# Four edits to a planned one-core kernel: an eviction's engine, three ring buffers, the split of the warming matmuls, and a new order of the work

## The chip, the core and the metric

The kernel runs on one core of one Trainium2 chip. A core has five engines, each with a queue of its own that it works through in order: TensorE (PE: matrix multiplications, with its weight loads, PEld), VectorE (DVE), ScalarE (ACT), GpSimdE (POOL) and SyncE (SP, which here only issues transfers). [...] A matrix multiplication writes to one of eight accumulator banks (PSUM); ACT or DVE then copies the bank to on-chip memory, which is called an eviction here.

The metric is the time of one execution on the device in microseconds. Of the kernel before, three runs gave 339.36, 339.56 and 339.56 us: median 339.56.

## The reference

Two layers, each a long convolution and a gated feed-forward block, on one sequence of 2048 rows with 512 columns. What is computed:

```python
def A(q, k, v, shift_k, ssm_k, ssm_D):        # convolution
    k_shift = sum(k shifted down by j rows * shift_k[:, j] for j in 0..3)
    kv = k_shift * v
    y  = causal convolution over all 2048 rows of kv with ssm_k   # by FFT
    return q * (y + kv * ssm_D)

def B(x, w_gate, w_up, w_down):               # feed-forward, F = 1792
    return (silu(x @ w_gate) * (x @ w_up)) @ w_down

x = A_q
x = x + A(layernorm(x), ...);  x = x + B(layernorm(x), ...)
x = x + A(layernorm(x), ...);  x = x + B(layernorm(x), ...)
```

All inputs are bfloat16. The convolution's `y` does not depend on `x`, so it is computed once and used in both layers.

## The kernel before

**Tiles and stages.** The sequence is cut into four blocks `c` of 512 rows, a block into two halves `h` of 256 rows. A unit is `(layer, c, h)`: one half of one block in one layer, sixteen in all. For each unit a prologue normalises, multiplies with `y`, adds to `x`, normalises again and transposes the result to `zT`; `ffn` then multiplies `zT` with `wg_sb` and `wu_sb` (line 400 of the profile, written by `mm`), evicts on ACT (`sg`, `hr`, `ht`), multiplies on DVE, and multiplies with `wd_sb` (line 1200).

**The convolution** is done with matrix products in place of an FFT. For block 0, `transpose_h` turns the filter `hn` (line 567), `transpose_k` turns `kn` to `kTb` (line 456), `half` takes the filter's spectrum `ev` in eight matrix products of two terms each (slots a, b, c, d, two parts each), whose banks are evicted at line 509 (ACT) or 512 (DVE); `shift_mul` multiplies `kTb` by the diagonal matrices `dg` (the four taps, made at lines 1362 and 1366) and DVE multiplies the result by `v` (line 614); `direct` takes the spectrum `X0` of that (line 548). DVE forms `G0` from `ev` (lines 535, 537), then the products `t`, `Z` and sums `m` (lines 732, 736, 873), TensorE turns them back (line 879), and the first prologue follows (lines 990 to 1013), at whose end the first feed-forward product can start. `EVE` is the string that names the engine of each eviction of `half(hs, ev, ...)`: its first four letters belong to slots a and c, part 0 and 1 each.

**Strassen units.** In the five units named in `STRASSEN` some groups of the down product are done with seven products in place of eight (`seven`, line 1075). It needs sums of quarters of `wd_sb`, made once by `weight_sums` (lines 1035 and 1039): `wsa`, `wsb`, `wsc`, three of the eleven slots of the ring `s8` from then on.

**What sets the order.** Nothing is issued in the order in which the code is written. Each operation is put on a list with its engine, a cost and its readers and writers (`Plan.add`). `ORDER` is a table with one rank for each of the 1721 operations, written out by hand or by a search that is not in the kernel; `Plan.order` sorts by it, and each engine gets its operations in that order. `Plan.walk` then steps through the sorted list with the costs and gives every operation a planned start. The planned starts decide two things only: which slot of a ring a buffer gets, and where the warming matmuls go. No operation waits for its planned time on the chip; it waits for its operands and its slot.

**Warming matmuls** (`wm`, line 1485) multiply ones, so that TensorE is busy before its first data land. `Plan.issue` puts a run of them ahead of an operation of TensorE whose planned start is before 6.0 and over 0.5 after the planned end of the one before, as many as fit at 0.106 each, and then corrects the first run so that there are `WARM`, 33, in all:

```python
n = int((start - max(t, 0.3)) / 0.106)
...
fill[0][3] += WARM - sum(f[3] for f in fill)
```

In the code, the taps' transposes (line 1348) follow at 3.02 after the start (0.42 for the issue, 2.6 for landing) with a cost of 0.25, and the filter's (line 567) at 0.62 + `LH0`.

**Transfers** are issued by SP in the order of the table too: the filter, `k`, `v`, `x`, the weights, the inverse table `inv` by a transposing transfer, and later the transposes of `z` and of `hr`.

Of the kernel before, what the change touches and what calls it, by code (L numbers as in the profile page):

```python
# [33 lines left out]
LH0 = 4.0  # L34
# [7 lines left out]
EVE = "ADADAAAA"  # L42
# [80 lines left out]

PASSES, WARM, FETCH, PHASE, TOOK = 4, 33, 256, 173, 1.1

NS = 8
BLOCKS = [("C", 0, 1), ("C", 1, 1), ("C", 2, 1), ("C", 3, 1),
# [1389 lines left out]
```

## Time and profile before

| | us |
|---|---|
| median of three runs | 339.56 |
| the profiled execution's own time | 340.1 |
| its span, first to last instruction | 338.3 |
| TensorE busy | 333.9 |
| VectorE busy | 299.8 |
| ScalarE busy | 265.0 |
| GpSimdE busy | 34.5 |

The profiled execution took 340.1 us, of which 1.8 us lie around its span, and it is 0.54 us above the median. A busy time is the time in which at least one instruction of that engine was under way. Consecutive matrix products overlap: one of 512 columns is shown with 0.38 us, but the next can start 0.216 us later. So a busy TensorE is not one that issues without a gap; gaps are read from the starts of consecutive rows. In rows of the timeline stand start, length, engine, line, operation, tiles, and how many instructions of that kind are merged; in square brackets the idle time of the engine before it, and what ended it. `PEld` rows are weight loads, rows with a `q` are issues of transfers.

### The profile page before, as it was taken

The numbers are of one execution on the slowest core, as the hardware profiler recorded it, in microseconds if no ns is written. First come the engines' busy times: TensorE is split into PE (matmuls) and PEld (weight loads), VectorE is DVE, ScalarE is ACT, GpSimd is POOL, SyncE is SP. The second block draws the span as 40 slices with busy tenths as digits, with TensorE's granted clock in tenths as the row PEclk, the third lists the DMA queues.
The fourth block names the chain that finished last, engine by engine and source line by source line (L and its number), as shares of the span: only waits on it lengthen the run. The fifth ranks groups of instructions, "written<-read, shape, count | busy, mean of one in ns | idle before, by whom it ended". The sixth has DMA issues, their size and how long they took to land.

```text
span 338.3 us, 5940 instructions
## 1 busy us (share of the span) xinstructions
PE 333.9 (99%) x2172; PEld 205.7 (61%) x2172; DVE 299.8 (89%) x508; ACT 265.0 (78%) x543; POOL 34.5 (10%) x48
## 2 busy tenths in 40 slices
PE   9999999999999999999999999999999999999996
PEld 8665865645454564745444564644546587867884
DVE  7899999999779997999999999989997967977465
ACT  6989999999987477989999886989765555566473
POOL 4010011003100000132030000101200010100000
PEclk9999999999999999999999999999999999999999
DMA  7999501443355336381333263510504230203201
GB/s 266 341 290 365 75 0 33 84 107 90 64 125 93 81 79 155 62 159 32 62 48 67 57 107 116 105 34 16 96 16 96 56 85 2 48 17 78 64 3 62
DMA packets 77992, 31.59 MB, mean 93 GB/s; under 512 B 69765, under 2 KB 75786, under 8 KB 77962
## 3 DMA queue, kind: packets, MB, share of 16 engines
q1 hardware_dynamic: 77808, 31.13, 39.8%
q8 instruction: 17, 0.28, 0.3%
q14 instruction: 13, 0.11, 0.1%
q10 hardware_dynamic: 154, 0.07, 0.1%
HBM read 12.33 MB, written 2.10 MB: 43 GB/s over the span
## 4 chain that ended last, share of the span: by engine, by line
PE 87%; ACT 7%; DVE 5%; issue 1%; POOL 0%; DVEq 0%; POOLq 0%
PE pf L400 50%; PE pd L1200 17%; PE ps L1075 7%; PE ps L400 7%; PE ps L548 2%; ACT jk L922 2%; PE wm L1485 1%; PE ps L879 1%; ACT sg L1113 1%; ACT hr L1114 1%; ACT X L509 1%; PE pt L567 1%; DVE t L746 1%; DVE m L630 1%; DVE Z L750 1%; DVE t L742 1%
## 5 line engine op out<-in xcount | busy, mean ns | idle before, releaser
L400 PEld LDWEIGHTS <-zT 128*128 128x128 bf16 x528 | 51.5, 98 | 59.4 <-DMA zT<-z 0.9
L400 PE MATMUL pf<-wu_sb,zT 128*128 128x512 bf16 x264 | 65.0, 379 | 0.0
L400 PE MATMUL pf<-wg_sb,zT 128*128 128x512 bf16 x264 | 64.9, 379 | 0.0
L1200 PE MATMUL pd<-wd_sb,sg 128*128 128x512 bf16 x200 | 49.4, 379 | 0.0
L1113 ACT ACTIVATE sg<-pf 128x512 bf16<-128x512 f32 x66 | 38.7, 604 | 11.4 <-PE pf L400 10.3
L400 PE MATMUL pf<-zT,wg_sb 128*128 128x256 bf16 x368 | 46.7, 273 | 0.0
L1114 ACT CAST hr<-pf 128x512 bf16<-128x512 f32 x66 | 38.2, 591 | 9.6 <-PE pf L400 9.0
L400 PE MATMUL pf<-zT,wu_sb 128*128 128x256 bf16 x368 | 45.4, 273 | 0.2 <-ACT zT L1013 0.2
L742 DVE TENSOR_TENSOR t<-X,G 128x4096 bf16<-128x4096 bf16 x18 | 41.0, 2280 | 0.1
L400 PEld LDWEIGHTS <-wg_sb 128*128 128x128 bf16 x368 | 36.0, 98 | 8.0
L400 PEld LDWEIGHTS <-wu_sb 128*128 128x128 bf16 x368 | 36.0, 98 | 7.1 <-issue 0.5
L1173 ACT ACTIVATE sg<-pf 128x512 bf16<-128x512 f32 x46 | 27.5, 606 | 10.9 <-PE pf L400 9.7
L1177 ACT CAST ht<-pf 128x512 bf16<-128x512 f32 x46 | 27.3, 599 | 10.8 <-PE pf L400 10.4
L889 POOL TENSOR_TENSOR rstd<-mv,nhalf 128x2 f32<-128x2 f32 x20 | 18.5, 928 | 160.3 <-DVE mv L899 160.3
L1200 PEld LDWEIGHTS <-sg 128*128 128x128 bf16 x200 | 19.6, 98 | 21.5
L1200 PE MATMUL pd<-wd_sb,ht 128*128 128x512 bf16 (+1 forms) x126 | 29.1, 369 | 0.0
L898 DVE BATCH_NORM_STATS2 bst<-xc 128x6 f32<-128x512 bf16 x40 | 26.4, 682 | 0.5
L1180 DVE TENSOR_TENSOR ht<-ht,sg 128x512 bf16<-128x512 bf16 (+1 forms) x31 | 16.7, 546 | 9.5 <-ACT sg L1173 6.2
L889 POOL TENSOR_TENSOR rstd<-ve,nhalf 128x2 f32<-128x2 f32 x12 | 12.4, 1032 | 112.3 <-ACT ve L926 112.3
L1120 DVE TENSOR_TENSOR hr<-hr,sg 128x1024 bf16<-128x1024 bf16 x27 | 18.4, 681 | 4.3 <-ACT hr L1114 2.3
L509 ACT ACTIVATE X<-ps 128x512 bf16<-128x512 f32 x32 | 18.8, 611 | 2.2 <-DVE Z L746 1.1
L1200 PEld LDWEIGHTS <-ht 128*128 128x128 bf16 x126 | 12.3, 98 | 12.8 <-ACT z L945 0.3
(143 smaller groups left out, 525.7 us busy)
## 6 DMA issues: line engine op xcount, KB each, us to landing
hn<-in_A_ssm_k_dram SPq DMA_DIRECT2D x4, 512.0 KB, 4.0
vt<-in_A_v_dram SPq DMA_DIRECT2D x4, 512.0 KB, 6.0
xc<-in_A_q_dram SPq DMA_DIRECT2D x4, 512.0 KB, 5.3
out_dram<-xc SPq DMA_DIRECT2D x15, 128.0 KB, 1.8
wg_sb<-in_B_w_gate_dram SPq DMA_DIRECT2D x1, 1792.0 KB
wu_sb<-in_B_w_up_dram SPq DMA_DIRECT2D x1, 1792.0 KB, 7.9
wd_sb<-in_B_w_down_dram SPq DMA_DIRECT2D x1, 1280.0 KB, 13.2
sg<-hr SPq DMA_TRANSPOSE x66, 2.4
```

What stands on the lines that cost most here:

```text
L400: nc.tensor.matmul(o, lhsT=lhsT, rhs=rhs, start=(n == 0), stop=(n == len(terms) - 1))
L509: add("ACT", act(D), lambda: nc.scalar.activation(out=view(), in_=ps.t[:], func=ACT.Copy, scale=scale), r=[ps], w=[(buf, keys)], conv=conv)
L742: dve(8 * D, lambda t=t, part=part: nc.vector.tensor_mul(out=t.t[:], in0=x.t[:, :, part:part + 1, :].to_broadcast((P, R, 2, D)), in1=g.t[: ...
L889: add("POOL", cost, lambda: nc.gpsimd.tensor_tensor(out=rstd.t[:], in0=var(), in1=nhalf.t[:].to_broadcast((P, n)), op=ALU.pow), r=reads + ...
L898: add("DVE", 0.6, lambda st=st, i=i: nc.vector.bn_stats(out=st.t[:, 0:6], in_=xs[c].t[:, i, :]), r=[(xs[c], (i,))], w=[st])
L1075: nc.tensor.matmul(bank.t[:, half_ * C:(half_ + 1) * C], lhsT=lhsT(i), rhs=rhs(i), start=(first and i == 0 and half_ == 0), stop=(last and ...
L1113: add("ACT", act(D), lambda ps=ps, dst=dst, o=o, which=which: nc.scalar.activation(out=rows(dst, o), in_=ps.t[:], func=ACT.Silu) if which ...
L1114: out=rows(dst, o), in_=ps.t[:], func=ACT.Silu) if which == "g" else nc.scalar.copy(out=rows(dst, o), in_=ps.t[:]),
L1120: dve(n * W, lambda: nc.vector.tensor_mul(out=hr.t[:], in0=hr.t[:], in1=sg.t[:]), [sg], [hr], due=(unit, k / pairs, 0.0, "h"))
L1173: add("ACT", act(D), lambda ps=ps, o=o, sg=sg: nc.scalar.activation(out=sg.t[:, o:o + 2, :], in_=ps.t[:], func=ACT.Silu), r=[ps], w=[(sg, ...
L1177: add("ACT", act(D), lambda ps=ps, o=o, ht=ht: nc.scalar.copy(out=ht.t[:, o:o + 2, :], in_=ps.t[:]), r=[ps], w=[(ht, (o // 2,))], due=(uni ...
L1200: nc.tensor.matmul((pds[o] if not cs.start else pds[HP]).t[:, cs], lhsT=ht.tiles(q, o), rhs=wt["d"].t[:, ft, cs], start=(ft == std0 and no ...
```

## The change

1. `LH0` goes from 4.0 to 3.85, and `Plan.walk` counts an operation of TensorE that starts before `RAMP`, 5.4, at up to 1.92 times its cost. Both are numbers of the plan; through it they set where the warming matmuls go (33 in all, as before) and which slots buffers get.
2. `EVE` goes from `ADADAAAA` to `AAADAAAA`: the eviction of slot a, part 1 of the filter's spectrum goes from DVE (line 512) to ACT (line 509).
3. `weight_sums` writes its five results to five buffers: two in the rings `h` and `k` (one slot each, earlier used for the filter and for `kTb`), one in `hs`, one in `dg` (a ring of one slot now, for the diagonals), and one in `s8`. The last two take sums of even and of odd tiles in place of first and second halves. `seven` reads them under new names.
4. `ORDER` is replaced. Of 523 operations of TensorE 437 stand at another position in its queue, of 508 of DVE 399, of 497 of ACT 433, of 43 of POOL 18 and of 150 of SP 91. The sets of operations are the same, but for the eviction of item 2.

```diff
-LH0 = 4.0
+LH0 = 3.85
...
-EVE = "ADADAAAA"
+EVE = "AAADAAAA"
...
 ORDER = [
-    1, 64, 179, 187, 2, 5, 0, 11, 15, 3, 4, 8, 14, 34, 36, 9, 7, 10, 6, 13, 19, 18, 17, 16, 20, 25, 27, 45, 51, 41, 47, 48, 31, 55, 33, 42, 32, 39,
...
+    6, 53, 44, 124, 2, 7, 4, 12, 24, 1, 3, 0, 17, 18, 30, 10, 8, 11, 9, 15, 27, 21, 19, 16, 20, 29, 32, 34, 40, 31, 56, 78, 22, 46, 14, 36, 23, 49,
...
 ]
...
-PASSES, WARM, FETCH, PHASE, TOOK = 4, 33, 256, 173, 1.1
+PASSES, WARM, FETCH, PHASE, TOOK, RAMP = 4, 33, 256, 173, 1.1, 5.4
...
             o.end = o.start + o.cost
+            if o.eng == "PE" and o.start < RAMP:
+                o.end += 0.48 * min(1.92 * o.cost, RAMP - o.start)
...
-    plan = Plan({"h": 1, "k": 1, "v": 1, "hs": 1, "x": 2, "y": 2, "s8":11, "n": 2, "jk": 1, "dn": 1, "ks": 2, "z": 3, "zT":3,
+    plan = Plan({"h": 1, "k": 1, "v": 1, "hs": 1, "dg": 1, "x": 2, "y": 2, "s8":11, "n": 2, "jk": 1, "dn": 1, "ks": 2, "z": 3, "zT":3,
...
-    dg = whole("dg", [P, KD, KS, P], parts=KD * KS)
+    dg = new("dg", "dg", [P, KD, KS, P], parts=KD * KS)
...
-        a = ws["14"] = new("s8", "wsa", [P, 2, NF // 2, C], parts=2)
-        b = ws["3"] = new("s8", "wsb", [P, NF // 2, C])
-        c = ws["67"] = new("s8", "wsc", [P, NF, C])
...
+        a0, a1 = (new(ring, "wsa", [P, NF // 2, C]) for ring in ("h", "k"))
+        b = new("hs", "wsb", [P, NF // 2, C])
+        c0, c1 = (new(ring, "wsc", [P, NF // 2, C]) for ring in ("dg", "s8"))
+        ws.update({"1": a0, "4": a1, "3": b, "6": c0, "7": c1})
...
```

The heads of the queues, as they follow from the two tables:

| queue | before | after |
|---|---|---|
| TensorE | taps; filter rows 3, 0, 1, 2; `kn` parts 3, 1, 2, 0; spectrum c, c, a, a; `dg` products and spectrum b, d | taps; filter rows 2, 0, 1, 3; `kn` 0, 1, 2; spectrum b, a, c, d; `kn` 3; `dg` products and the other four of the spectrum |
| DVE, from the taps' copies on | tapT, tapF, phases, three `dg`, a row of `hs`, both negated tables, a row of `hs`, five `dg`, `kTb`, ev, `kTb`, ev, G, four `vt` | tapF, phases, negated table, `dg`, negated table, tapT, two rows of `hs`, six `dg`, `kTb`, `dg`, `kTb`, ev, G, four `vt` |
| ACT, around the spectrum | two `kTb`, ev, `dg`, ev, `dg`, two ev, sums of `x` | `kTb`, ev, `kTb`, ev, `dg`, three ev, sums of `x` |
| POOL | iota, iota, `ident`, zeros of `kTb`, ... | iota, zeros of `kTb`, iota, `ident`, ... |
| SP, after `wd_sb` part 1 of 2 | `wd_sb` part 2, `xc` of block 1, `hn` of block 2, `kTb` of block 2, ...; `vt` of block 2 much later | `hn` and `vt` of block 2, `wd_sb` part 2, `xc` of block 1, `kTb` of block 2, ... |

Up to the first feed-forward product TensorE has the same operations to do in both tables, in another order. In both, the last ten operations of TensorE, the last seven of DVE and the last three of ACT are the same.

More of the change, by code (lines that the diff above doesn't have):

```diff
@@ L1027, in weight_sums @@
         lo, hi = slice(0, C), slice(C, D)
-        a = ws["14"] = new("s8", "wsa", [P, 2, NF // 2, C], parts=2)
-        b = ws["3"] = new("s8", "wsb", [P, NF // 2, C])
-        c = ws["67"] = new("s8", "wsc", [P, NF, C])
-        for out, keys, x0, x1, op in (
-                (lambda: a.t[:, 0], [(a, (0,))], lambda: ev(lo), lambda: od(hi), ALU.add),
-                (lambda: b.t[:], [b], lambda: ev(hi), lambda: od(hi), ALU.subtract),
-                (lambda: a.t[:, 1], [(a, (1,))], lambda: od(lo), lambda: ev(lo), ALU.subtract)):
-            dve(NF // 2 * C, lambda out=out, x0=x0, x1=x1, op=op: nc.vector.tensor_tensor(out=out(), in0=x0(), in1=x1(), op=op),
-                [wd], keys)
-        for n in range(2):
-            sl = slice(n * NF // 2, (n + 1) * NF // 2)
-            dve(NF // 2 * C, lambda sl=sl: nc.vector.tensor_tensor(out=c.t[:, sl], in0=wd.t[:, sl, lo], in1=wd.t[:, sl, hi], op=ALU.add),
-                [wd], [c])
+        a0, a1 = (new(ring, "wsa", [P, NF // 2, C]) for ring in ("h", "k"))
+        b = new("hs", "wsb", [P, NF // 2, C])
+        c0, c1 = (new(ring, "wsc", [P, NF // 2, C]) for ring in ("dg", "s8"))
+        ws.update({"1": a0, "4": a1, "3": b, "6": c0, "7": c1})
+        for out, x0, x1, op in ((a0, lambda: ev(lo), lambda: od(hi), ALU.add), (b, lambda: ev(hi), lambda: od(hi), ALU.subtract),
+                                (a1, lambda: od(lo), lambda: ev(lo), ALU.subtract), (c0, lambda: ev(lo), lambda: ev(hi), ALU.add),
+                                (c1, lambda: od(lo), lambda: od(hi), ALU.add)):
+            dve(NF // 2 * C, lambda out=out, x0=x0, x1=x1, op=op: nc.vector.tensor_tensor(out=out.t[:], in0=x0(), in1=x1(), op=op),
+                [wd], [out])
     def strided(src, off, dims):
@@ L1060, in seven @@
         for bank, rd, terms in (
-                (e, [ht, ws["14"], ws["3"]], (
-                    (0, lambda i: ht.tiles(2 * i + 1, 1), lambda i: ws["14"].t[:, 1, f0 + i]),
+                (e, [ht, ws["4"], ws["3"]], (
+                    (0, lambda i: ht.tiles(2 * i + 1, 1), lambda i: ws["4"].t[:, f0 + i]),
                     (1, lambda i: ht.tiles(2 * i, 0), lambda i: ws["3"].t[:, f0 + i]))),
@@ L1066, in seven @@
                     (1, lambda i: cb.t[:, 1, i], lambda i: wd.t[:, 2 * (f0 + i), 0:C]))),
-                (r, [(cb, (1,)), ws["67"]], (
-                    (0, lambda i: cb.t[:, 3, i], lambda i: ws["67"].t[:, 2 * (f0 + i) + 1]),
-                    (1, lambda i: cb.t[:, 2, i], lambda i: ws["67"].t[:, 2 * (f0 + i)]))),
-                (o, [(cb, (2,)), ws["14"]], (
-                    (0, lambda i: cb.t[:, 4, i], lambda i: ws["14"].t[:, 0, f0 + i]),))):
+                (r, [(cb, (1,)), ws["6"], ws["7"]], (
+                    (0, lambda i: cb.t[:, 3, i], lambda i: ws["7"].t[:, f0 + i]),
+                    (1, lambda i: cb.t[:, 2, i], lambda i: ws["6"].t[:, f0 + i]))),
+                (o, [(cb, (2,)), ws["1"]], (
+                    (0, lambda i: cb.t[:, 4, i], lambda i: ws["1"].t[:, f0 + i]),))):
             def go(bank=bank, terms=terms):
```

126 rows, old and new, of the table ORDER are left out of this document.

## The prediction

> **What bounds the kernel now.** I read the page's sums and chain first, then busy time by stage, then the timeline wherever TensorE is not issuing.
>
> ```profile
> span 338.3 us, 5940 instructions
> ...
> PE 333.9 (99%) x2172; PEld 205.7 (61%) x2172; DVE 299.8 (89%) x508; ACT 265.0 (78%) x543; POOL 34.5 (10%) x48
> ...
> PE 87%; ACT 7%; DVE 5%; issue 1%; POOL 0%; DVEq 0%; POOLq 0%
> ```
>
> The last of these rows is the chain that ended last: TensorE holds 87% of it. The change removes no matmul, so all it can win is time in which TensorE does not issue, or issues slowly. By stage (stretch, its length, then busy time and count of PE, PEld, DVE, ACT, POOL, granted clock, DMA):
>
> ```profile
> 8.00:12.00 4.00, 4.00 (x45) 2.87 (x44) 3.30 (x7) 3.94 (x9) 0.00 (x0) 1.00 1.04 398
> 26.40:33.20 6.80, 6.33 (x57) 3.72 (x56) 6.25 (x16) 6.80 (x15) 0.78 (x1) 1.00 1.08 364
> 255.00:338.30 83.30, 80.27 (x640) 62.35 (x637) 58.61 (x147) 46.84 (x88) 4.66 (x6) 1.00 0.22 50
> ```
>
> From 8 to 12 ScalarE is the fullest engine beside TensorE; from 26.4 to 33.2 TensorE loses 0.47 even by busy time; in the last 83 us it lacks only what lies at the very end. Now the start, from the timeline and two answers on single tiles (shortest, median and longest matmul in ns; issue to landing of the filter's loads):
>
> ```profile
> 0.77 2.40 PE L1485 MATMUL wm<-const-bfloat16-1.0 128*128 128x128 bf16 x21 [0.77 <-PEq L1503]
> 3.10 0.29 PE L1348 MATMUL pt<-ident,tapR 4*128 4x4 bf16 x4
> 3.32 1.46 PE L1485 MATMUL wm<-const-bfloat16-1.0 128*128 128x128 bf16 x12
> 4.58 1.91 PE L567 MATMUL pt<-ident,hn 128*128 128x128 bf16 x16
> 6.29 1.40 PE L456 MATMUL pt<-ident,kn 128*128 128x128 bf16 x16
> 10.79 3.07 PE L400 MATMUL ps<-dg,kTb 128*128 128x128 bf16 x52
> ...
> L456 PE MATMUL pt<-ident,kn x16: 219/219/311, 6.3 to 7.5; 128*128 128x128 bf16 x16
> ...
> DMA to landing us min/median/max: 3.6/5.7/7.8
> ```
>
> The granted clock is 1.00 in every stretch, yet the pitch is not: sixteen filter transposes take 1.91, less the last one's 0.31 is 1.60 for 15 steps, 0.107 each; 52 later ones take 3.07, less 0.22 is 2.85 for 51 steps, 0.056. TensorE runs at half rate early. The `kn` row holds the change: 1.40 less 0.22 is 1.18 for 15 steps, some seven slow and eight fast, so it comes near 7.0. Sixteen plus seven useful matmuls are slow by 0.051 each: 1.2 us lost. The filter landed at 0.74 + 3.6 = 4.34; TensorE took it up at 4.58.
>
> The end of the head, where the first feed-forward product waits, and the unit of pitch (the last row, from the chain: 20 matmuls of 512 columns in 4.32, 0.216 each):
>
> ```profile
> 25.43 2.31 PE L879 MATMUL ps<-m,inv 128*128 128x512 bf16 x9
> 31.10 0.38 PE L879 MATMUL ps<-m,inv 128*128 128x512 bf16 x1
> 31.78 0.72 PE L1008 MATMUL ptz<-ident,z 128*128 128x128 bf16 x8 [0.31 <-DVE z L950]
> 32.44 0.60 PE L400 MATMUL ps<-vt,fwd 128*128 128x512 bf16 x2
> 33.22 1.91 PE L400 MATMUL pf<-zT,wu_sb 128*128 128x256 bf16 x16 [0.17 <-ACT zT L1013]
> ...
> 65.11 4.32 PE pd L1200 x20
> ```
>
> Nine in 2.31 need 8 x 0.216 + 0.38 = 2.11: 0.20 idle. From 31.10 + 0.216 to 31.78 are 0.46, after eight transposes (0.45) 0.21, after two matmuls (0.43) 0.35. The head loses 1.2 us of issue, and ends when `zT` is there: a chain over VectorE from `ev` through G, `vt`, the products, the normalisation and `z`.
>
> The stalls of the long middle, with the two waits behind them (total us, times, longest):
>
> ```profile
> 240.23 2.32 PE L1200 MATMUL pd<-wd_sb,sg 128*128 128x512 bf16 x10
> 242.53 1.04 PE L400 MATMUL pf<-wg_sb,zT 128*128 128x512 bf16 x4
> 251.60 1.30 PE L400 MATMUL ps<-Z,inv 128*128 128x512 bf16 x4
> 252.74 1.03 PE L1200 MATMUL pd<-wd_sb,sg 128*128 128x512 bf16 x4
> ...
> PEld L400 <- DMA zT<-z: 0.9, 2, 0.5
> PEld L400 <- DVE Z L647: 0.6, 1, 0.6
> ```
>
> 240.23 + 2.16 = 242.39 to 242.53: 0.14. 251.60 + 0.86 = 252.46 to 252.74: 0.28. With the other of the two waits for `zT`, some 0.1, the middle loses 0.5 us in 300. So all that can be won is 1.2 (half rate) + 1.2 (head) + 0.5 (middle), under 1% of the time; what can be lost has no such limit, since every queue is reordered.
>
> **The change, part by part.**
>
> *Warming run.* The count stays 33; only the split moves. By the code, before: taps at 3.02 give int(2.72/0.106) = 25, then the filter at 4.62 less 3.27 gives 12; 37 is four too many, so 21 and 12, as the rows show. After: 25 for the taps; with the ramp the taps end at 3.02 + 0.25 + 0.23 = 3.50, the filter is due at 4.47: int(0.97/0.106) = 9; 34 is one too many: 24 and 9. On the chip the first 21 go at (2.40 - 0.31)/20 = 0.1045, so 24 are through at 0.77 + 24 x 0.1045 = 3.28, and the taps go 0.18 later. From the taps to the filter were 4.58 - 3.10 = 1.48; three warm ones fewer make 1.16: filter at 4.45, after its landing at 4.34. That (3.28 + 1.16 = 4.44, say 4.45) is 0.13 earlier, 1.2 slow matmuls, worth 0.07 if the rate changes at the same moment. Bounds: 0 and 0.24 (4.58 to 4.34). The taps' 0.18 goes on to the `dg` tiles, which are read only after the filter and the first spectrum products; I take it as hidden, at most 0.18.
>
> *Rate early.* That the plan counts half rate changes nothing on the chip by itself. [...]
>
> *The eviction to ScalarE, and the new head.* Rows: groups by line (busy, mean ns), then the timeline.
>
> ```profile
> L509 ACT ACTIVATE ev<-ps 128x512 bf16<-128x512 f32 x6 | 3.5, 601 | 0.3 <-PE ps L400 0.3
> L512 DVE TENSOR_SCALAR ev<-ps 128x512 bf16<-128x512 f32 x2 | 1.4, 688 | 0.4 <-PE ps L400 0.4
> ...
> 10.33 1.25 ACT L509 ACTIVATE ev<-ps 128x512 bf16<-128x512 f32 x2
> ...
> 11.01 0.69 DVE L537 TENSOR_TENSOR G<-ev 128x1024 bf16<-128x1024 bf16 x1
> ...
> 11.88 2.70 DVE L614 TENSOR_TENSOR vt<-ps,vt 128x512 bf16<-128x512 f32 x4 [0.18 <-PE ps L400]
> ```
>
> VectorE gives up 0.69, in a stretch where it idles 0.70 of 4 us anyway; ScalarE takes on 0.60 where it has 0.06 to spare. G waits for the four evictions of slots a and c. In the new order the last of their products, slot c part 0, stands behind four filter and four `kn` transposes, six spectrum products and two `dg` products: from 4.45, 24 slow steps of 0.107, sixteen fast of 0.056 and twelve of 0.216 end at 10.5; its eviction, taken as 0.2 behind (`vt` waits 0.18 for TensorE), ends at 11.3, and so G starts at 11.3 against 11.01. But `vt` behind it waits for TensorE, and the work ahead of its first row is the same in both orders (six spectrum products, seven `dg` products, all transposes): about 11.8, so VectorE, free at 12.0, comes to `vt` some 0.1 late. Its work from there to `z` is the same: +0.1, between -0.2 (the 0.18 that `vt` waits) and +0.6 (ScalarE's whole eviction handed on).
>
> At the far end the `zT` copy now stands ahead of another eviction on ScalarE, and the last inverse product is put behind the transposes: -0.1, between 0 and the 0.35 that TensorE waited there. Head: 0.
>
> *The weight sums.* Five operations of VectorE before and after, of one width; the rings they move to are empty by then, since filter, `k` and diagonals of the last block have been read.
>
> ```profile
> L1035 DVE TENSOR_TENSOR wsa<-wd_sb 128x1792 bf16<-128x1792 bf16 x2 | 2.2, 1084 | 0.0
> ...
> L1039 DVE TENSOR_TENSOR wsc<-wd_sb 128x1792 bf16<-128x1792 bf16 x2 | 2.2, 1084 | 0.0
> ```
>
> The sums over alternate tiles (`wsa`) and those over halves (`wsc`) cost the same already: 0, either way. Two slots of `s8` come free from the first sum on. That is worth something only where a buffer is late; the last 83 us have no stall for it to remove. 0, at best the 0.4 of the middle.
>
> *SP's queue.* Block 2's filter and `v` go ahead of the second part of `wd_sb`.
>
> ```profile
> 19.67 1.05 SPq L484 DMA_DIRECT2D wd_sb<-in_B_w_down_dram  x2
> ...
> 20.18 1.89 PE L548 MATMUL ps<-vt,fwd 128*128 128x512 bf16 x8
> ...
> wd_sb<-in_B_w_down_dram SPq DMA_DIRECT2D x1, 1280.0 KB, 13.2
> ...
> 47.17 1.03 PE L1200 MATMUL pd<-wd_sb,ht 128*128 128x512 bf16 x4
> ...
> 50.00 2.51 SPq L980 DMA_TRANSPOSE zT<-z  x2
> ```
>
> `v` needs the slot that the spectrum products leave at 22.07, so the second part is issued near 22.7, not 20.2, behind 1 MB more (2.9 us at the 364 GB/s of that stretch): it lands at 22.7 + 13.2 + 2.9 = 38.8, and its first product, the second group's, is at 47.17. Hidden, with 8 us of cover. The transposes of `z` behind it start at 50.00. Were the cover gone, each microsecond would be one of TensorE.
>
> *POOL.* The zeros of `kTb` move ahead of an iota that the phases need:
>
> ```profile
> 1.63 0.22 POOL L450 MEMSET kTb<- 128x64 bf16 x1
> ...
> 3.01 0.62 ACT L1320 ACTIVATE fwd<-ph 128x512 bf16<-128x512 int32 x1
> ```
>
> 0.22 later at most; the sine at 3.01 is behind ScalarE's table load and has as much to spare. 0.
>
> *The middle's new order.* New stalls are unknown. Below, all 0.5 gone; above, as much as the head loses, 1.2, once more. I take 0.3, nearest to what the same kinds of wait cost now: -0.2.
>
> **Sum.** 340.1 - 0.07 (start) + 0.0 (head) - 0.2 (middle) = 339.8 for a profiled execution. This one lay 0.54 above the median 339.56, so the median comes to 339.3.
>
> **Rivals.** *The head shortens.* The order, made for slow early transposes, brings `ev`, `vt` and `z` early enough that two thirds of the head's 1.2 and the middle's 0.5 go: 339.56 - 1.1 = 338.4. For it: VectorE, which carries that chain, is freed of 0.69, and the first spectrum products no longer wait for the last `kn` transposes. Against: TensorE's work ahead of `vt` is unchanged, VectorE's after it too.
>
> *ScalarE becomes the bound of the head (slower).* In 8 to 12 it has 0.06 us free and gets 0.60. If the evictions of the spectrum queue behind it, G, `vt` and each product's bank come up to 0.6 late, and the sums of `x` behind them too; with 0.5 of new stalls in the middle: 339.3 + 1.1 = 340.4. It decides once the last of the four evictions ends after 11.8, when the first `vt` could start. Against: the first spectrum products now stand ahead of the last `kn` transposes, so ScalarE gets its first bank sooner.
>
> *The slow stretch ends earlier.* The pause of the warming matmuls around the taps, from 0.77 + 21 x 0.1045 = 2.96 to 3.32, shrinks from 0.36 to the taps' own 0.22. If that lets the rate change before the filter, the 23 slow matmuls win 1.2: 338.1. Against: a pause stays, and the first 0.77 us stay empty. [...]
>
> *Nothing comes of it* is my forecast within its bounds.
>
> **Chances.** A change under 0.2% (0.68 us, about what can be told from none here) is the forecast: 0.48, own range 338.9 to 340.2. Head shortens: 0.24. Slow stretch ends earlier: 0.06. Slower, by ScalarE or by new stalls of the middle: 0.22. So faster 0.30, same 0.48, slower 0.22. The range, 338.2 to 340.6, takes in the rivals' times.
>
> **What would show it.** 24 and 9 warming matmuls; taps near 3.3, filter near 4.45; G near 11.3 and `vt` near 12.0; first feed-forward product at 33.0 to 33.4 with about 1.2 of gaps before it; gaps of 0.1 to 0.5 after it. I am wrong if that product comes before 32.6 or after 33.9, or if the middle has gaps over 1 us.

## The result, and the profile after

The changed kernel takes 341.28 us (median of six runs, 341.12 to 341.52), the kernel before 339.62 in the same comparison (six runs, 339.36 to 340.66). The ratio is 1.0045, interval 1.0032 to 1.0058: slower by 0.45%, outside the predicted range of 338.2 to 340.6.

The profiled execution took 341.52 us with a span of 339.7, against 340.1 and 338.3 before. The page's sums and its chain (shares of the span by engine):

```profile
PE 333.5 (98%) x2172; PEld 204.9 (60%) x2172; DVE 299.7 (88%) x507; ACT 264.2 (78%) x544; POOL 35.5 (10%) x48
...
PE 89%; DVE 5%; ACT 3%; POOL 1%; DMA 1%; issue 1%
```

Every engine is busy as long as before, within 0.8 us, except GpSimdE (POOL), which is busy 1.0 longer. POOL has 1% of the chain where it had none. The busy times of one stretch, first of the kernel before and then of the changed one (stretch, its length, then busy time and count of PE, PEld, DVE, ACT, POOL, granted clock, DMA), show where the time went:

```profile
55.00:75.00 20.00, 20.00 (x117) 11.21 (x115) 19.83 (x23) 19.27 (x41) 1.80 (x2) 1.00 0.33 68
```

```profile
55.00:75.00 20.00, 18.20 (x107) 10.24 (x106) 17.43 (x21) 17.18 (x38) 5.80 (x2) 1.00 0.33 67
```

In these 20 us TensorE, VectorE and ScalarE each lose about 2 us of work, and POOL alone is busy longer, by 4.0 us with the same two instructions. (Over the whole span POOL gains only 1.0, since it is 3.0 shorter elsewhere; the total alone does not show the place.) The timeline of TensorE in the changed kernel:

```profile
60.82 1.91 PE L402 MATMUL pf<-zT,wg_sb 128*128 128x256 bf16 x16
62.57 0.38 PE L402 MATMUL ps<-hs,fwd 128*128 128x512 bf16 x1
64.51 1.03 PE L402 MATMUL pf<-zT,wu_sb 128*128 128x256 bf16 x8 [1.56 <-ACT sg L1111]
65.69 1.03 PE L402 MATMUL pf<-zT,wu_sb 128*128 128x256 bf16 x8 [0.15 <-ACT sg L1171]
66.56 3.01 PE L1198 MATMUL pd<-wd_sb,sg 128*128 128x512 bf16 x12
```

A product of 512 columns allows the next after 0.216 (eight from 69.41 to 71.14), one of 256 after 0.109 (the sixteen from 60.82 to 62.57). From 62.57 + 0.22 to 64.51 are 1.72 us without an issue, from 64.51 + 8 x 0.109 to 65.69 are 0.31, and the twelve in the last row take 3.01 where 11 x 0.216 + 0.38 = 2.76 would do: 0.25. Together 2.28 us, in a place where the kernel before has no stall. The bracket says that ScalarE's eviction `sg` was late. Why, the chain of the changed kernel tells in order of time (start, length, what):

```profile
57.21 0.30 ACT ve L928
...
57.59 5.04 POOL rstd L891
...
62.65 0.30 ACT nmr L940
...
62.98 0.81 ACT n L947
...
63.98 0.49 ACT sg L1111
```

`rstd`, the reciprocal root of a layer normalisation, is one instruction on two numbers a partition. It takes 5.04 us here. ScalarE's `nmr` needs it and starts at 62.65, after 2.72 of idle time; the evictions `sg` stand behind `nmr` in ScalarE's queue and wait too (by the timeline they start at 63.88 and 65.06), and TensorE, which needs the banks that they empty, waits 1.56 and 0.15 for them. Its neighbours on POOL and VectorE (start, length, ...), in the kernel before and in the changed one:

```profile
57.37 0.99 POOL L889 TENSOR_TENSOR rstd<-ve,nhalf 128x2 f32<-128x2 f32 x1 [9.97 <-ACT ve L926]
...
57.13 0.68 DVE L636 TENSOR_TENSOR X<-m 128x1024 bf16<-128x1024 bf16 x1
57.84 2.29 DVE L742 TENSOR_TENSOR t<-X,G 128x4096 bf16<-128x4096 bf16 x1
60.05 0.68 DVE L1120 TENSOR_TENSOR hr<-hr,sg 128x1024 bf16<-128x1024 bf16 x1
```

```profile
57.59 5.03 POOL L891 TENSOR_TENSOR rstd<-ve,nhalf 128x2 f32<-128x2 f32 x1 [10.93 <-ACT ve L928]
...
55.84 1.22 DVE L748 TENSOR_TENSOR Z<-t,t 128x2048 bf16<-128x2048 bf16 x1
56.98 2.28 DVE L744 TENSOR_TENSOR t<-X,G 128x4096 bf16<-128x4096 bf16 x1
59.18 0.69 DVE L1118 TENSOR_TENSOR hr<-hr,sg 128x1024 bf16<-128x1024 bf16 x1
59.78 2.29 DVE L744 TENSOR_TENSOR t<-X,G 128x4096 bf16<-128x4096 bf16 x1
```

All these VectorE instructions read two operands from on-chip memory, as `rstd` does. Compare start plus length with the next start. Before, `X<-m` ends at 57.81, `t` starts at 57.84, a pause of 0.03, and `rstd` ends at 58.36, 0.55 after 57.81. In the changed kernel each start lies 0.08 ahead of the previous end, so the products form an unbroken row, which ends at 59.78 + 2.29 = 62.07; `rstd` ends at 62.62, again 0.55 later. Elsewhere an undisturbed `rstd` takes 0.69 (at 95.83 of the changed kernel, with VectorE idle). The order before has `Z` two products earlier; the new order puts `t` right behind `Z`, which it does not depend on, and the pause is gone.

The rest agrees with the sum of the two executions: the first feed-forward product comes at 32.60 instead of 33.22 (0.62 earlier, for a reason that is not the change, see below), the new stall costs 2.28, the other stalls of the middle fall by some 0.2. That makes +1.5, and 341.52 - 340.1 is 1.4.

### The profile page after: what moved, and what is told of

The parts are those of the page before. It is cut to its first block, busy times and chain, and to the rows that moved or that the text cites. A ratio compares the mean times of both kernels' runs of the same rounds, so it can differ in the third digit from the quotient of the medians.

```text
span 339.7 us, 5935 instructions
## 1 busy us (share of the span) xinstructions
PE 333.5 (98%) x2172; PEld 204.9 (60%) x2172; DVE 299.7 (88%) x507; ACT 264.2 (78%) x544; POOL 35.5 (10%) x48
## 4 chain that ended last, share of the span: by engine, by line
PE 89%; DVE 5%; ACT 3%; POOL 1%; DMA 1%; issue 1%
PE pf L402 54%; PE pd L1198 20%; PE ps L1073 7%; PE ps L402 6%; POOL rstd L891 1%; DVE t L734 1%; PE wm L1483 1%; DVE Z L738 1%; DMA sg<-hr 1%; DVE m L875 1%; PE pt L569 0%; DVE bst L900 0%; ACT jk L924 0%; DVE G L537 0%; ACT sg L1111 0%
## 5 line engine op out<-in xcount | busy, mean ns | idle before, releaser
L402 PE MATMUL pf<-zT,wu_sb 128*128 128x256 bf16 x368 | 46.1, 272 | 1.8 <-ACT sg L1111 1.6
L891 POOL TENSOR_TENSOR rstd<-mv,nhalf 128x2 f32<-128x2 f32 x20 | 16.7, 835 | 150.5 <-DVE mv L901 139.5
L1198 PE MATMUL pd<-wd_sb,ht 128*128 128x512 bf16 (+1 forms) x126 | 29.9, 369 | 0.0
L891 POOL TENSOR_TENSOR rstd<-ve,nhalf 128x2 f32<-128x2 f32 x12 | 15.2, 1268 | 121.5 <-ACT ve L928 121.5
```

The source lines that it names most:

```text
L402: nc.tensor.matmul(o, lhsT=lhsT, rhs=rhs, start=(n == 0), stop=(n == len(terms) - 1))
L891: add("POOL", cost, lambda: nc.gpsimd.tensor_tensor(out=rstd.t[:], in0=var(), in1=nhalf.t[:].to_broadcast((P, n)), op=ALU.pow), r=reads + ...
L1198: nc.tensor.matmul((pds[o] if not cs.start else pds[HP]).t[:, cs], lhsT=ht.tiles(q, o), rhs=wt["d"].t[:, ft, cs], start=(ft == std0 and no ...
```

## The experiments

The first theory, A: VectorE's unbroken row of two-operand products holds `rstd`, ScalarE stands behind `rstd`, TensorE behind ScalarE. Rivals: `rstd` is slow for some other reason (R); the transposing transfers on SP's queue make the stall (Q); the eviction on ScalarE or the buffers of the sums cost by themselves (B). A diff on `ORDER` is written here as the place where an instruction goes. All experiments but e4 and those on the kernel before start from the changed kernel.

**e1: `t` later**

```diff
 VectorE, 57 to 65 us
  t<-X,G          (56.98)
  hr<-hr,sg       (59.18)
- t<-X,G          (59.78)
  hr<-hr,sg       (64.49)
+ t<-X,G
```

> The changed kernel with one instruction moved: VectorE's second product t<-X,G of the pair at 57 to 62 us goes behind the next product hr<-hr,sg. Theory A (the reciprocal root rstd on GpSimd, 5.03 us at 57.59, is kept from finishing by VectorE's two-input products that run one right behind the other until 62.07; ScalarE stands behind it, and TensorE behind ScalarE): rstd ends about 0.55 us after the end of hr<-hr,sg, near 60.4 instead of 62.62, the TensorE gaps between 62 and 68 us fall from 2.3 to under 0.5, and the time is 339.0 to 339.6. Rival R (rstd is slow for another reason, VectorE beside it is chance): rstd stays near 5 us, time 341.3. Rival Q (the queue of DMA transposes, hr ahead of sg, makes the stall): the gap that ends with sg from a DMA stays, 0.3 to 0.6 us, time 340.3 to 340.8.

Measured: 341.1 us (341.0 to 341.24), ratio to the kernel before 1.0047 (1.003 to 1.0063). `rstd` as predicted, the time not. POOL, VectorE and TensorE:

```profile
57.63 2.82 POOL L891 TENSOR_TENSOR rstd<-ve,nhalf 128x2 f32<-128x2 f32 x1 [10.94 <-ACT ve L928]
...
59.22 0.69 DVE L1118 TENSOR_TENSOR hr<-hr,sg 128x1024 bf16<-128x1024 bf16 x1
62.33 0.69 DVE L1118 TENSOR_TENSOR hr<-hr,sg 128x1024 bf16<-128x1024 bf16 x1 [2.42 <-ACT sg L1111]
62.94 2.28 DVE L744 TENSOR_TENSOR t<-X,G 128x4096 bf16<-128x4096 bf16 x1
...
64.57 2.84 PE L1198 MATMUL pd<-wd_sb,sg 128*128 128x512 bf16 x11
69.06 0.60 PE L1198 MATMUL pd<-wd_sb,ht 128*128 128x512 bf16 x2 [1.64 <-DVE ht L1178]
```

The row ends at 59.91, `rstd` at 60.45, and the stall at 62.6 is gone: theory A holds for `rstd`, and R falls. But VectorE now spends 59.9 to 62.3 waiting and does the moved `t` after it, so `ht` comes late, and TensorE stands 1.8 us at 67. The gain was given back one wait later.

**e2: what needs `rstd` stands behind the next evictions**

```diff
 ScalarE, 60 to 66 us
- nmr, n, nmr
  sg (L1111)
- n
  sg (L1171)
+ nmr, n, nmr, n
```

> The changed kernel with ScalarE's queue changed at 60 to 65 us: the four instructions that need rstd (two nmr, two n) stand behind the next two sg evictions instead of ahead of them. VectorE's and GpSimd's queues are those of the changed kernel. Theory A: rstd is still about 5 us long, but ScalarE evicts sg at about 59.9 and 60.5 instead of 63.88 and 65.06, the gaps of TensorE between 62 and 68 us fall from 2.3 to under 0.6, and the time is 339.0 to 339.8. Rival Q (TensorE waits for the transposes of hr and sg and not for ScalarE standing): the gaps stay over 1.5 us, time 341 or more. If the n that come later than before hold up VectorE (its n<-n,Yk at 65.19) the gain is given back at 70 us and the time is 340.5 to 341.3.

Measured: 341.84 us (341.55 to 343.36), ratio 1.0076 (1.0053 to 1.0099). The stall at 62.57 is gone, with `rstd` longer than ever, so what carried it to TensorE was ScalarE's queue, and rival Q falls. The expectation's last case came true, and a little beyond:

```profile
57.71 5.62 POOL L891 TENSOR_TENSOR rstd<-ve,nhalf 128x2 f32<-128x2 f32 x1 [10.95 <-ACT ve L928]
...
62.09 0.69 DVE L1118 TENSOR_TENSOR hr<-hr,sg 128x1024 bf16<-128x1024 bf16 x1
65.57 0.69 DVE L974 TENSOR_TENSOR n<-n,Yk 128x1024 bf16<-128x1024 bf16 x1 [2.79 <-ACT n L947]
...
69.50 1.04 PE L1198 MATMUL pd<-wd_sb,ht 128*128 128x512 bf16 x4 [2.09 <-DVE ht L1178]
```

The row is now one product longer (it ends at 62.78) and `rstd` with it (63.33). VectorE waits 2.79 for `n`, and TensorE 2.09 for `ht`. A late `rstd` has two users; moving one of them hands the delay to the other.

**e3: `t`, `t`, `hr` in place of `t`, `hr`, `t`**

```diff
 VectorE
  t<-X,G          (56.98)
- hr<-hr,sg       (59.18)
  t<-X,G          (59.78)
+ hr<-hr,sg
```

> The changed kernel with two instructions of VectorE exchanged: the products run t, t, hr instead of t, hr, t. rstd starts beside the first t as before. Theory A in its strict form (rstd is not let through at the border of two VectorE products that follow each other without a pause): rstd ends 0.55 us after the last of the unbroken row, 62.0 to 62.7, and the time stays 341.0 to 341.5. Theory A in its loose form (let through at the end of the first product, as at 147 and 174 us of the kernel before, and kept out here by something special to the border of t and hr): rstd ends near 59.8, time 339.0 to 339.6.

Measured: 342.73 us (342.66 to 342.88), ratio 1.0094 (1.0079 to 1.0109). `rstd` takes 5.03 us again, from 57.59, and ends 0.55 behind the end of the row of three (62.08). So no particular border inside the row is to blame. The time is worse than the strict form said, by 1.2, since with the later `hr` another wait comes at 69 (VectorE's `ht` starts at 69.66, after 1.20 of idle time).

**e4: the changed code with the order of before**

```diff
-    6, 53, 44, 124, 2, 7, 4, 12, 24, 1, 3, 0, 17, 18, 30, 10, 8, 11, 9, 15, 27, 21, 19, 16, 20, 29, 32, 34, 40, 31, 56, 78, 22, 46, 14, 36, 23, 49,
...
+    1, 64, 179, 187, 2, 5, 0, 11, 15, 3, 4, 8, 14, 34, 36, 9, 7, 10, 6, 13, 19, 18, 17, 16, 20, 25, 27, 45, 51, 41, 47, 48, 31, 55, 33, 42, 32, 39,
...
```

> The changed kernel's code (h eviction on ScalarE, the buffers of the weight sums, the warming constant) with the order table of the kernel before. Theory A (the loss sits in the new order at 57 to 68 us alone): no gap over 0.5 us between 40 and 250 us, time 338.9 to 339.8. Rival B (the eviction on ScalarE or the buffers of the sums cost by themselves): 340.3 to 341.5.

Measured: 339.7 us (339.21 to 340.0), ratio 1.0007 (0.9997 to 1.0016). The eviction on ScalarE, the buffers of the sums and the split of the warming matmuls together make no difference that can be told. Rival B falls: the loss lies in the order alone.

**e5: `ve` earlier.** In all traces so far an `rstd` that starts within 0.25 us of a product's start was let through at that product's end, even if another followed at once (at 147.62 and 174.87 in the kernel before, for instance, 2.77 and 2.57 long). Is it the moment of asking that decides?

```diff
 ScalarE, 55 to 58 us
- sg (L1111)
  jk, ve
+ sg (L1111)
```

> The changed kernel with one eviction of ScalarE (sg, at 55.88) moved behind the three short instructions that end in ve, so that ve is ready 0.5 us earlier. rstd then starts near 57.1, about 0.1 us after VectorE's first t<-X,G (56.98) instead of 0.61 us after it. Theory A, strict (rstd is let through only where VectorE pauses): it stays until 62.1 and ends near 62.6, about 5.5 us long, time 340.9 to 341.5. Theory A, by the moment of asking (in the traces so far an rstd that starts within 0.25 us of a VectorE product is let through at the end of that product, also where the next follows at once; the one that starts 0.61 us after it is not): rstd ends at about 59.8, the four ScalarE instructions behind it come 2.8 us earlier, no gap over 0.5 us on TensorE from 60 to 72 us, time 338.8 to 339.5.

Measured: 341.65 us (341.39 to 341.67), ratio 1.0059 (1.0039 to 1.0079).

```profile
57.25 5.42 POOL L891 TENSOR_TENSOR rstd<-ve,nhalf 128x2 f32<-128x2 f32 x1 [10.54 <-ACT ve L928]
```

`rstd` starts 0.21 after `t` (57.04) and is still held to the row's end (62.12). The moment does not decide.

**e6: a pause behind `t`**

```diff
...
                 op = nc.vector.tensor_mul(
                     out=t.t[:], in0=x.t[:, :, part:part + 1, :].to_broadcast((P, R, 2, D)), in1=g.t[:])
+                if at == PAUSE:
+                    op = nc.vector.tensor_copy(out=scr.t[:], in_=t.t[:, 0, 0, 0:1])
...
```

`at` is the operation's number in the table, `PAUSE` that of this `t`.

> The changed kernel with one tiny instruction added: behind VectorE's first t<-X,G at 56.98 stands a copy of one column of its result into a scratch tile, which has to wait for that product and so makes a pause of some 0.03 us; nothing else is changed, and the copy's result is not used. Theory A, strict or not (a pause lets rstd through): rstd ends near 59.8 instead of 62.62, TensorE's gap at 62.57 goes, and the ht product that TensorE needs at 67 us comes no later than before, since neither VectorE nor ScalarE waits for rstd beyond 60: time 338.8 to 339.5. If the hold has nothing to do with pauses: rstd ends at 62.7, time 341.3 to 341.6. If the gain is given back at a next wait, as at 67 us where the product t or the n were only moved: 340.5 to 341.5 with a gap over 1.5 us near 67 us.

Measured: 339.11 us (338.7 to 339.46), ratio 0.9983 (0.9974 to 0.9992): 2.2 us less than the changed kernel for one more instruction, and faster than the kernel before.

```profile
57.43 2.22 POOL L901 TENSOR_TENSOR rstd<-ve,nhalf 128x2 f32<-128x2 f32 x1 [10.95 <-ACT ve L938]
...
56.82 2.28 DVE L749 TENSOR_TENSOR t<-X,G 128x4096 bf16<-128x4096 bf16 x1
59.13 0.16 DVE L752 COPY scr<-t 128x1 bf16<-128x1 bf16 x1
59.20 0.68 DVE L1128 TENSOR_TENSOR hr<-hr,sg 128x1024 bf16<-128x1024 bf16 x1
```

`t` ends at 59.10, the copy that needs it starts 0.03 later, and `rstd` ends at 59.65, 0.55 after 59.10. All later waits moved up with it: from 61 to 70 us TensorE's rows follow each other without a pause. This shows that the hold on `rstd` is the whole loss.

**e7: the kernel before, with `ve` behind two casts**

```diff
 ScalarE, 56 to 58 us
- ve
  hr, ht
+ ve
```

> The kernel before, with ve moved behind the next two casts of ScalarE's queue, so that rstd starts near 58.3, some 0.5 us into VectorE's product t<-X,G (57.84 to 60.13), and not at 57.37 in the short product ahead of a pause. Theory A (an rstd that starts late in a long product of an unbroken row is held to the end of the row): rstd is over 4 us long, ends at 63.4 to 64.1 behind the row of t, hr, t, hr, ScalarE waits for it, and the kernel before takes the loss of the changed kernel: 341.0 to 342.5. If rstd is let through at the end of the product: it ends near 60.7, 0.5 us behind the nmr that used it at 60.15, time 339.4 to 340.0.

Measured: 339.81 us (339.37 to 340.48), ratio 1.0006 (0.9996 to 1.0016): the loss does not come.

```profile
57.30 2.48 POOL L889 TENSOR_TENSOR rstd<-ve,nhalf 128x2 f32<-128x2 f32 x1 [10.80 <-ACT ve L926]
...
56.23 0.68 DVE L636 TENSOR_TENSOR X<-m 128x1024 bf16<-128x1024 bf16 x1
56.94 2.29 DVE L742 TENSOR_TENSOR t<-X,G 128x4096 bf16<-128x4096 bf16 x1
59.15 0.69 DVE L1120 TENSOR_TENSOR hr<-hr,sg 128x1024 bf16<-128x1024 bf16 x1
```

This is the run that changed the theory. `hr` follows `t` without a pause, as in the changed kernel, and yet `rstd` ends at 59.78, 0.55 after the end of `t`. What is different lies ahead: `t` is the first product after a pause here (56.91 to 56.94). Theory B: an `rstd` that starts in the first product of a row gets through at its end; one that starts in a later product is held to the end of the row. It agrees with e1 to e3 and e5, and the next three runs test it.

**e8: the pause ahead of `t`**

```diff
...
                 op = nc.vector.tensor_tensor(
                     out=out.t[:, :, part], in0=t1.t[:, :, part], in1=t2.t[:, :, 1 - part], op=comb)
+                if at == PAUSE:
+                    op = nc.vector.tensor_copy(out=scr.t[:], in_=out.t[:, 0, part, 0:1])
...
```

> The changed kernel with a tiny copy of one column (result unused) ahead of VectorE's first t<-X,G at 56.98, behind Z<-t,t, instead of behind that product. It ends the unbroken row of two-input products before t, and makes no pause after it. Theory B (an rstd that starts in the first product of a row gets through at the end of that product, one that starts in a later product of the row is held to the row's end): rstd is about 2.2 us long and ends near 59.9, time 338.8 to 339.5 as with the pause behind t. Theory A, strict (only a pause after the product lets it through): rstd is 5 us long and ends near 62.8, time 341.2 to 341.8.

Measured: 339.44 us (338.79 to 339.65), ratio 0.9988 (0.9979 to 0.9998). `t` (57.37) is now the first product behind the copy and ends at 59.65, and `hr` follows it without a pause:

```profile
57.79 2.41 POOL L900 TENSOR_TENSOR rstd<-ve,nhalf 128x2 f32<-128x2 f32 x1 [10.93 <-ACT ve L937]
```

`rstd` ends 0.55 after `t`, as theory B says, and no pause behind `t` was needed.

**e9: the kernel before, with `Z` moved to where the change has it**

```diff
 VectorE
- Z<-t,t          (55.39)
  X<-m            (56.52)
  X<-m            (57.13)
+ Z<-t,t
  t<-X,G          (57.84)
```

> The kernel before with one instruction of VectorE moved: Z<-t,t (55.39) goes two products later, between X<-m (57.13) and t<-X,G, as it stands in the changed kernel. The pause of 0.03 us between X<-m and t goes with it, so that X, X, X, Z, t, hr, t, hr run as one unbroken row in which rstd starts at about 57.4. Theory B: rstd is held to the end of the row and ends at 63.4 to 64.1, over 5.5 us long; ScalarE and TensorE wait, and the kernel before takes the loss: 340.8 to 342.5. If the loss of the changed kernel had another cause than this row: rstd ends at 58.4 to 60.8, time 339.3 to 340.0.

Measured: 344.18 us (342.32 to 344.67), ratio 1.0121 (1.009 to 1.0151). One instruction moved two places costs the kernel before more than the whole change did.

```profile
57.30 5.99 POOL L889 TENSOR_TENSOR rstd<-ve,nhalf 128x2 f32<-128x2 f32 x1 [9.97 <-ACT ve L926]
...
61.37 1.04 PE L400 MATMUL pf<-zT,wg_sb 128*128 128x256 bf16 x8
65.18 3.37 PE L400 MATMUL pf<-zT,wu_sb 128*128 128x256 bf16 x16 [2.77 <-ACT sg L1113]
```

`rstd` is held until 63.29, TensorE stands 2.9 us (61.37 + 8 x 0.109 = 62.24 to 65.18), and the sixteen products after that take 3.37 where sixteen of this kind take 1.91 at 60.82 of the changed kernel; of this below. Even more than the 342.5 expected, since no theory had that second loss.

**e10: the changed kernel, with `Z` moved back**

```diff
 VectorE
+ Z<-t,t
  X<-m            (54.64)
  X<-m            (55.24)
- Z<-t,t          (55.84)
  t<-X,G          (56.98)
```

> The changed kernel with that same instruction moved the other way: Z<-t,t (55.84) goes ahead of the two X<-m, so that t<-X,G stands right behind the X<-m whose result it reads, with a pause of 0.03 us ahead of it, as in the kernel before. No instruction is added. Theory B: rstd starts in the first product of a row, ends near 59.9, TensorE's gaps between 60 and 72 us stay under 0.5 us in all, time 338.7 to 339.4, faster than the kernel before by 0.1 to 0.3 per cent. If only a pause after the product helps: rstd 5 us, time 341.0 to 341.6.

Measured: 339.57 us (338.72 to 339.77), ratio 0.9991 (0.9982 to 1.0001). `t` stands behind a pause again, `rstd` gets through at its end, and the stretch of the first section reads, for this kernel:

```profile
57.80 2.35 POOL L891 TENSOR_TENSOR rstd<-ve,nhalf 128x2 f32<-128x2 f32 x1 [10.93 <-ACT ve L928]
...
57.32 2.29 DVE L744 TENSOR_TENSOR t<-X,G 128x4096 bf16<-128x4096 bf16 x1
...
55.00:75.00 20.00, 20.00 (x118) 11.43 (x117) 19.76 (x25) 19.57 (x42) 3.12 (x2) 1.00 0.44 93
```

TensorE is full again. Nothing was added, and one instruction has moved two places. The same edit in both directions (e9, e10) makes and unmakes the loss, so the cause is shown.

Without the hold the change is worth 0.1 to 0.2%: e6, e8 and e10, which differ only in how they let `rstd` through, stand at 0.9983, 0.9988 and 0.9991. That a version with a pause beats both kernels is shown by e6 and e8, whose intervals stay under 1; for e10 it just does not.

What stays open: why twelve of the eighteen `rstd` that start in a later product get through all the same. In the twelve traces of this case `rstd` starts 140 times in a row's first product with another right behind it, and gets through at that product's end every time. It starts 18 times in a later one with another right behind it: six times it is held (the changed kernel, e1, e2, e3, e5 and e9), twelve times it isn't: at 37 to 38 us in `vt<-ks,vt` (0.42 long) under the old order, and at 16 us in `t<-X,G` (0.69 long) under the new one. The held ones start in products of 1.22 and 2.28, which are the seventh or eighth of their row (the small `nm`, 0.15 long, counted in); the others start in the fourth or fifth. Whether the length of the product or its place in the row decides wasn't tried. So theory B explains the place where the loss arises, and is not a rule for every row.

## Why the prediction was wrong

**The step that failed: "The middle's new order. New stalls are unknown [...] above, as much as the head loses, 1.2, once more. I take 0.3."** In the sum it stood as -0.2, 0.3 us of stalls for the 0.5 of before. Measured, the stalls of the middle are 2.3 us at 62.6 to 68 and 0.3 elsewhere, so the term is +2.1. What stands in its place is the hold on `rstd`, handed on by ScalarE's queue. Both the value and the upper bound were too small, because both were taken from the kinds of wait that cost something before (`zT`, `Z`), and this one cost nothing before. The profile of before had a row that bears on it and that I did not quote, the durations of `rstd` there (shortest, median and longest in ns):

```profile
L889 POOL TENSOR_TENSOR rstd<-ve,nhalf x12: 683/840/2767, 17.3 to 238.2; 128x2 f32<-128x2 f32 x12
```

An instruction on two numbers whose time runs from 0.68 to 2.77 is waiting for something inside its own time, where no view counts a wait. The new order could be read for what it puts beside each `rstd`; behind `ve` it has the row `t`, `hr`, `t`, 5.1 us by the rows of before (2.29, 0.68 and 2.29, each 0.08 into the next). That would have been a better upper bound than 1.2.

**The slower rival named the wrong place.** "ScalarE becomes the bound of the head" did not happen. VectorE in the changed kernel:

```profile
10.88 0.69 DVE L539 TENSOR_TENSOR G<-ev 128x1024 bf16<-128x1024 bf16 x1 [0.65 <-ACT ev L511]
11.49 1.91 DVE L616 TENSOR_TENSOR vt<-ps,vt 128x512 bf16<-128x512 f32 x3
```

G still waits for ScalarE, but starts at 10.88 and `vt` at 11.49, ahead of the 11.3 and 12.0 predicted; the evictions that G needs were over before 11.8, the point from which that rival decides. The 0.22 given to slower did include "new stalls of the middle", with 0.5 for them; they were 2.3.

**The warming run: the split right, the gain not.** There are 24 and 9 matmuls, as forecast:

```profile
0.77 2.72 PE L1483 MATMUL wm<-const-bfloat16-1.0 128*128 128x128 bf16 x24 [0.77 <-PEq L1501]
3.42 0.29 PE L1346 MATMUL pt<-ident,tapR 4*128 4x4 bf16 x4
3.64 1.14 PE L1483 MATMUL wm<-const-bfloat16-1.0 128*128 128x128 bf16 x9
4.81 1.47 PE L569 MATMUL pt<-ident,hn 128*128 128x128 bf16 x16
```

The taps come at 3.42, not at 3.3. Before, they start 0.14 behind the end of the warming matmuls (2.96 to 3.10), and the sum left that out; 3.28 + 0.14 is 3.42. With it the filter comes to 3.42 + 1.16 = 4.58, where it started before, and not to 4.45: the 33 matmuls and the taps take as long in either split. It does start at 4.58 in e1, e2 and e5. In the changed kernel's profile it came at 4.81, 0.24 after the last warming matmul allowed it (4.47 + 0.107), since its transfer landed late (issued at 0.73, it took 4.0, where it took 3.6 in the profile of before), and with the new split it lies anywhere from 4.32 (e6) to 4.99 (e10). The 0.07 of the sum was a slip, too small to matter.

**The head at 0: near in size, partly by luck.** The first product came at 32.60, at the limit given and ahead of the 33.0 to 33.4 forecast. That is 0.6 earlier than in the profile of before, and it isn't the change: under the old order the same product starts at 32.70 in e4, 32.32 in e7 and 33.13 in e9, under the new one at 32.46 (e6) to 32.83 (e10). The two orders can't be told apart by it. What varies is the start: read from the steps of 128-column matmuls (0.107 at the slow rate, 0.056 at the fast one), the half rate ends anywhere from 3.7 us or just before (e3, e6) to 7.0 (the kernel before), under either order; it ends at 5.7 in the changed kernel. The three runs of the kernel before lay 0.2 apart (339.36 to 339.56), but ten runs of one kernel lie 0.8 apart (e4, 339.21 to 340.0).

**"The slow stretch ends earlier": it does in some executions, and not through the change.** The rate changes before the filter in e3, e6 and e7 (in e7 the filter's transposes run at 0.056 from 4.58 on). The reason that the rival gave, a shorter pause around the taps, does not hold: e7 has the warming run of before. There the first feed-forward product starts at 32.32 against 33.22, so what the rival priced at 1.2 comes to at most 0.9 between these two executions. Its 338.1 also lay just outside the range that was said to take in the rivals' times.

**The rest of the change at 0: right.** e4 shows it for the code: 1.0007. And once the hold is gone, the new order comes to 339.1 to 339.6, around the forecast of 339.3. From the first feed-forward product to the start of the last matmul the kernel before takes 301.8 us, e4 301.9 and e7 302.0; e6 301.5, e8 301.3 and e10 301.8; the changed kernel 303.8. So one term failed, apart from the 0.07, and that one was left to a bound.

## What to carry to other kernels

When an order is replaced, look up every small instruction of an engine that shares something with a neighbour, compare its shortest with its longest time, and ask what the new order puts beside it; the longest time that a row of neighbours allows is the bound (5.1 us here, where 1.2 was taken), not the stalls that exist now. An instruction that waits inside its own time shows up as busy (`rstd` with 5.03 us, where it takes 0.69 beside an idle VectorE), so look for an engine that is busy longer with the same work. A dependence that makes an engine pause for 0.03 us may be what lets another engine in (`rstd` takes 2.35 us with that pause in e10, 5.03 without it); before moving an independent instruction into that place, see who uses the pause.

## What the runs showed of the hardware

**A row of two-operand products on VectorE held a POOL instruction past several of its members.** `rstd` ends 0.55 us after the end of the product that lets it in, in every case listed here: 2.2 to 2.5 us long when held by one product of 2.28 (e6, e7, e8, e10), 2.82 by two (e1), 5.03 to 5.42 by three (the changed kernel, e3, e5), 5.62 by four (e2), 5.99 from `Z` on (e9). What `rstd` waits for can be the second or third product after the one that it met (the second in the changed kernel, the third in e2). In the other direction the runs show no such hold: in e6 `hr` starts at 59.20, while `rstd` runs until 59.65, and takes 0.68 as elsewhere.

**After a stall of 2.9 us TensorE came back at half rate.** In e9 the granted clock around the stall (same columns as above) reads:

```profile
60.00:64.00 4.00, 2.41 (x16) 1.37 (x14) 2.74 (x2) 0.86 (x3) 3.29 (x1) 1.00 0.48 97
64.00:66.00 2.00, 0.82 (x5) 0.56 (x5) 0.35 (x1) 2.00 (x5) 0.00 (x0) 0.70 0.00 0
66.00:68.00 2.00, 2.00 (x11) 1.40 (x10) 1.92 (x4) 2.00 (x5) 0.00 (x0) 0.50 0.22 45
68.00:70.00 2.00, 2.00 (x16) 1.47 (x15) 1.66 (x5) 1.54 (x4) 0.60 (x1) 0.95 0.43 87
```

The sixteen products from 65.18 on take 3.37 - 1.91 = 1.46 us more; at a clock of 0.50, which doubles the 0.109, that is some thirteen of them (an estimate, 1.46 / 0.109). The stalls of 1.7 us (the changed kernel), 1.8 (e1) and 2.2 (e2) cost no such thing, the clock stays at 1.00 from 62 to 68 us of the first and from 66 to 72 of the other two. The drop comes in some executions only, by the mean granted clock of each of e9's four: 0.995 in those of 343.93 to 344.67 us, 0.999 in the one of 342.32, which lies in the range that was expected without it.
